# Ten idle products, an earlier gate, ScalarE as second asker for weights, and tables made by GpSimd, around the first routing of an attention and two-expert-layer kernel

## The chip, the cores and the metric

The kernel runs on one core of one Trainium2 chip. A core has TensorE (PE, matrix products; PEld is its loading of the stationary operand), VectorE (DVE), ScalarE (ACT), GpSimd (POOL) and SyncE (SP), which asks for most transfers. The metric is the time of one execution on the device in microseconds (us), as the median of several runs.

## The reference, cut to what matters

Attention over 2 x 8 heads of 576 tokens keeps the 32 largest scores of each row. Its output is an x of 1152 rows of 512. Two layers of eight experts follow, each with a gate that sends a row to one expert:

```python
logits = x @ w_gate
expert_idx = np.argmax(logits, axis=1)
...                                   # gate_w: the softmax value of the chosen expert
h = np.maximum(np.einsum('ecd,edf->ecf', disp, w1), 0.0)     # 512 -> 1024
y = np.einsum('ecf,efd->ecd', h, w2)                         # 1024 -> 512
...
        out[i] = gate_w[i] * y[expert_idx[i], pos[i]]
```

The first layer drops what an expert gets beyond its capacity of 288 rows; the second has no such limit. Only the routing depends on the data: which rows go to which expert.

## The kernel before, in words

**Stages.** Attention fills the first 249 us. At 249 us the first routing begins (`begin`, L1861): VectorE finds each row's expert and counts, experts are sorted by their number of rows, and rank 0 is the expert with most. From 256 us the first expert layer runs rank after rank, from about 412 us the second routing, and then the second expert layer to the end.

**Shapes.** The ranks of the first layer get 208, 192, 176, 160, 144, 128, 128 and 128 columns (L28), rows of x turned into columns. Rank 0 and 1 thus have two tiles of rows each (128 + 80 and 128 + 64), rank 2 has 128 + 48. What does not fit goes through a spill loop (`spill`, L1641) under a condition on a count `nblk` that every engine reads; the loop's code is jumped over when the count is zero.

**Form "S".** For ranks with more than 128 columns, weights and activations are split into a high part (ScalarE writes it, L1270 for weights) and a low part (VectorE subtracts, L1271), and TensorE makes a product with both parts (L1350, L1352 in the first layer of an expert, L1389, L1391 in the second). The result of one block f of 128 hidden columns goes back by ScalarE (`t`, L1322), VectorE (`s`, L1323), ScalarE (high part of `hT`, L1315) and VectorE (low part, L1316). There are eight f to an expert; the second product adds over all eight, so it wants `hT` of every f in turn. Weights reach the chip as `raw` tiles of 1 MB, two for w1 and two for w2 of an expert, in four buffers; their split copies are `w1c` and `w2c`.

**The early block.** One block of 128 rows of one expert was found during attention already. Its first layer (`early_hidden`, L1829) and second layer (`early_out`, L1838) are TensorE's work while the routing is computed elsewhere. Its gate value is made by `early_gate` (L1843, twelve small operations on GpSimd) and `early_sum` (L1856, one exponential on ScalarE over what `early_gate` left).

**Order.** Instructions of an engine run in the order in which the code is written; there is no scheduler. `layer1` (L1325) takes a list of side jobs and runs one of them ahead of each f from 1 to 7; other jobs, the splits of the weights, are handed along in the same list. In rank 0 the side jobs are: last early output and `early_sum`, `gate_in` (L1751), `next_places` (L1739, tables for the second routing), the rows of rank 1 with the request for its w1, and the early block's way out.

**Queues.** Weights are asked for by SP (L1229 for w1, L1241 for w2). Rows of x are fetched by indirect transfers that GpSimd issues (`bring`, L1212, instruction at L1218), into five `xr` buffers. GpSimd also writes the results `yr` of a rank to memory (L1773).

Of the kernel before, what the change touches and what calls it, by code (L numbers as in the profile page):

```python
# [16 lines left out]
OP = mybir.AluOpType  # L17
AX = mybir.AxisListType
PS = bass.MemoryType.PSUM
DR = bass.MemoryType.DRAM  # L20
SP = mybir.EngineType.SP

TOPK = 32
NEG = -1.0e30
# [9 lines left out]
NCOL = len(COLS[0])  # L34
# [19 lines left out]
def attn_moe_moe_kernel(ctx, tc, q, k, v, g1, w11, w12, capacity, g2, w21, w22, out):  # L54
    nc = tc.nc
# [4 lines left out]
    KF = F // 128  # L60
# [1099 lines left out]
    def moe(i, pools, src, lg, w1, w2, limit):  # L1160
# [5 lines left out]
        with ExitStack():  # L1166
# [7 lines left out]
            def new(shape, name, dt=F32):  # L1174
                return (consts if i == 0 and name in soonest else sm).tile(shape, dt, name=name)
# [54 lines left out]
                    got.append(raw)  # L1230
                return got

            def load_w2(e, late=False):
                w_ = w2[ds(e, 1)].rearrange("o (c p) f -> p (o c) f", p=128)
                got = []
                for h in range(2):
                    raw = wt.tile([128, KD, F // 2], F32, name="raw", bufs=4)
                    if late and h == 0:
                        nc.gpsimd.memset(raw[0:1, 0, 0:1], 0.0)
                    raw = raw.rearrange("p a b -> p (a b)").rearrange("p (c f) -> p c f", f=Dm)  # L1240
                    nc.sync.dma_start(raw, w_[:, h * KF // 2:(h + 1) * KF // 2])  # L1241
                    got.append(raw)
                return got

            def load_w2_apart(e):
                w_ = w2[ds(e, 1)].rearrange("o (c p) f -> p (o c) f", p=128)
                got = []
                for h in range(4):
                    raw = wt.tile([128, 2, Dm], F32R, name="w2c", bufs=12).bitcast(F32)
                    nc.sync.dma_start(raw, w_[:, h * KF // 4:(h + 1) * KF // 4])  # L1250
                    got.append(raw)
                return got
# [368 lines left out]
            def gate_rows():  # L1621
                tt(r3, isa[:, None].to_broadcast(b3), gcode[:, :, None, :].to_broadcast(b3), op=OP.mult)

            def chosen_one(r):
                return nc.values_load(eid0[0:1, 0:1] if i and r == 0 else eid[0:1, r:r + 1], engines=[SP], min_val=0,
                                      max_val=E - 1, skip_runtime_bounds_check_because="ranks are a permutation of the experts")

            def weights(r, j, gate=None):
                e = chosen_one(r)
                if j == 0:  # L1630
                    w1s[r] = [load_w1(e, gate=gate), {}]
                else:
                    w2s[r] = [load_w2_apart(e) if i == 0 and r == E - 1 else load_w2(e, i == 1 and r == 0), {}]

            def splits(r, j):
                w, form, f = ((w1s, form1, split_w1), (w2s, form2, split_w2))[j]
# [100 lines left out]
                        turn_out(yT, 0, 128, g, lambda yr: scatter(yr, 128, si, free=False))  # L1737

            def next_places():  # L1739
                okay = new([128, NCOL], "okay")  # L1740
                ts(okay, inv, 1.0, None, op0=OP.is_lt)
                for a, b, to in ((0, NCOL - 1, 0), (NCOL - 1, NCOL, LAST)):
                    ok, n = okay[:, a:b], b - a
                    cr = code[1][:, :, to:to + n]
                    stt(cr[:, 0], part.to_broadcast([128, n]), 64.0, ok, op0=OP.add, op1=OP.mult)
                    ts(cr[:, 1], iot[:, to:to + n], 128.0, -64.0, op0=OP.mult, op1=OP.add)
                    tt(cr[:, 1], cr[:, 1], ok, op=OP.mult)
                    bo = [128, n, E]
                    tt(revm[1][:, to:to + n], ok[:, :, None].to_broadcast(bo), rev[:, None, :].to_broadcast(bo), op=OP.mult)

            def gate_in():  # L1751
                pg = ps.tile([128, 512], F32, name="pi", bufs=1)
# [108 lines left out]
            def begin():  # L1861
                bank()
                choose(0, nch)
                early_hidden(0)
                count(0, nch)
                nc.scalar.activation(dl, dl, AF.Exp)
                none = new([128, 1], "none", U32)
                nc.gpsimd.memset(none, 0)
                yr = wk.tile([128, RW], F32, name="yr", bufs=3)
                gather(yr[:16, :Dm], none[:16])  # L1870
                two.prepare()
                for f in range(1, 5):
                    early_hidden(f)
                early_hidden(5, 0, KD // 2)
                weave(*ranking())
                weights(0, 0)
                assign()
                for j in range(2):
                    bring(j)
                for f in table["later"]:  # L1880
                    f()
                spill()
                weights(0, 1)
                for a, (r, t, m) in enumerate(cols):
                    if 0 < r < 3:
                        bring(a)
                early_gate()
                first_split = splits(0, 0)
                for f in first_split[:2]:
                    f()  # L1890
                yTs[-1] = wk.tile([128, KD, ny], F32, name="yT")
                early_out(0, 0, KF)
                early_out(1, 0, KF)
                xTs[0] = wk.tile([128, KD, 2, MOST], F32R, name="xT")
                for k, q in enumerate(tiles_of(0)):
                    rows_in(0, *q)
                for f in first_split[2:6]:
                    f()
                early_out(2, 0, KF)
                first_split[6]()  # L1900
                table["left"] = first_split[7:]
# [123 lines left out]
            def run(nxt=None):  # L2025
                if i == 0:
                    begin()
                rest = {0: splits(0, 1)}
                for r in range(E):
                    hTs[r] = wk.tile([128, KF, 2, MOST], F32R, name="hT", bufs=1)  # L2030
                    jobs, more_ = side(r, nxt), rest[r]
                    if i and r == 0:
                        more_ = [lambda p=p: [(split_high if p < 4 else split_low)(k) for k in w2_order[p]]
                                 for p in range(len(w2_order))]
                    if i == 0 and r == 0:
                        more_ = [lambda p=p, m=more_: [m[k]() for k in p] for p in
                                 ((), (0,), (1,), (2, 3), (4,), (5, 6), (7,))]
                    jobs = [(lambda p=p: [f() for f in p]) for p in
                            [jobs[k:k + 1] + more_[k:k + 1] for k in range(max(len(jobs), len(more_)))]]
                    layer1(form1[r], *w1s[r], xTs[r], hTs[r], sizes[r], form2[r] != "N", jobs)  # L2040
                    if r + 1 < E:
                        if r + 1 not in w1s:
                            weights(r + 1, 0)
                        weights(r + 1, 1)
                    if r + 3 < E:
                        for t, m in tiles_of(r + 3):
                            bring(first[r + 3] + t)
                    early, rest[r + 1] = splits(r + 1, 0), splits(r + 1, 1)
                    n_ = max(0, 11 - len(early))
                    if form2[r] == "R" and len(tiles_of(r)) == 1:  # L2050
                        n_ = KH
                    early, rest[r + 1] = early + rest[r + 1][:n_], rest[r + 1][n_:]
                    if i and r == 0:
                        early += [lambda q=q: rows_in(1, *q) for q in tiles_of(1)]
                    if form2[r] != "R":
                        yTs[r] = wk.tile([128, KD, ny], F32, name="yT")
                    each = end = None
                    kept_, place, put = [], ("pp", 4), rows(r)
                    if i and r == E - 1:
                        place = "pl", 1  # L2060
                        put = lambda *a: kept_.append(a)
                    if i and r == 0:
                        def each(d):
                            if d < 0:
                                gate_in()
                                place_of(0)
                                place_of(1)
                    if nxt and r == E - 1:
                        each, end = ending(yTs[r])
                        early += nxt.later()  # L2070
                    layer2(form2[r], *w2s[r], hTs[r], yTs.get(r), sizes[r], tiles_of(r), put, early, each, place)
                    if end:
                        nxt.late(end(nxt.ready, nxt.begun))
                    if r + 2 < E and form1[r + 1] != "N":
                        weights(r + 2, 0)
                if i:
                    spill()
                    for a in kept_:
                        rows(E - 1)(*a)
# [46 lines left out]
```

## Time and profile before

| what | value |
|---|---|
| median of 3 runs | 593.14 us (592.06 to 596.36) |
| profiled execution, its own time | 593.53 us |
| its span, first to last instruction | 591.9 us |
| mean granted TensorE clock | 0.99 |
| busy: PE / PEld / DVE / ACT / POOL | 572.0 / 542.8 / 476.5 / 418.7 / 263.9 us |
| DMA | 100.76 MB, mean 170 GB/s |

The time of an execution holds 1.6 us more than the span, work before the first and after the last instruction. Busy time of TensorE counts a product from its start to a modelled end, and products overlap, so a stretch where PE is all busy can still run at half the clock; the granted clock has to be read beside it.

### The profile page before, as it was taken

The numbers are of one execution on the slowest core, as the hardware profiler recorded it, in microseconds if no ns is written. First come the engines' busy times: TensorE is split into PE (matmuls) and PEld (weight loads), VectorE is DVE, ScalarE is ACT, GpSimd is POOL, SyncE is SP. The second block draws the span as 40 slices with busy tenths as digits, with TensorE's granted clock in tenths as the row PEclk, the third lists the DMA queues.
The fourth block names the chain that finished last, engine by engine and source line by source line (L and its number), as shares of the span: only waits on it lengthen the run. The fifth ranks groups of instructions, "written<-read, shape, count | busy, mean of one in ns | idle before, by whom it ended". The sixth has DMA issues, their size and how long they took to land.

```text
span 591.9 us, 13975 instructions
## 1 busy us (share of the span) xinstructions
PE 572.0 (97%) x4781; PEld 542.8 (92%) x4781; DVE 476.5 (81%) x1597; ACT 418.7 (71%) x1040; POOL 263.9 (45%) x590
## 2 busy tenths in 40 slices
PE   8999999999999999879999999999999999999994
PEld 5799999999999999779899999998998899999994
DVE  6999999999999999656878868642598688788750
ACT  6789998989898977427677777552365577878651
POOL 7768888988898797544220111010103302221010
PEclk9999999999999999989999989999999999999998
DMA  6530513161470190164987757786677767778660
GB/s 145 138 81 3 167 43 114 43 144 24 127 95 23 36 271 19 43 222 149 317 271 278 235 181 269 220 263 231 203 268 237 267 221 244 258 236 280 213 215 14
DMA packets 85168, 100.76 MB, mean 170 GB/s; under 512 B 33925, under 2 KB 46725, under 8 KB 85088
## 3 DMA queue, kind: packets, MB, share of 16 engines
q1 hardware_dynamic: 80160, 88.79, 48.6%
q0 software_dynamic: 3728, 10.70, 5.8%
q8 instruction: 40, 0.66, 0.5%
q10 hardware_dynamic: 1200, 0.30, 0.2%
q14 instruction: 40, 0.33, 0.2%
HBM read 86.51 MB, written 13.74 MB: 169 GB/s over the span
## 4 chain that ended last, share of the span: by engine, by line
PE 31%; DMA 10%; issue 7%; DVE 3%; POOL 1%; ACT 1%; POOLq 0%; SPq 0%; DVEq 0%; ACTq 0%
DMA out_dram<-yr,sidx 8%; PE pp L1389 6%; PE pp L1350 6%; PE pp L1336 3%; PE pp L1352 3%; PE pp L1391 3%; DMA raw<-in_moe_w_dram 1%; DVE w2c L1271 1%; PE pt L1300 1%; PE pl L1403 1%; PE pp L1385 1%; PE pp L1387 1%; PE pp L1386 1%; PE pp L1838 1%; PE pt L1440 1%
## 5 line engine op out<-in xcount | busy, mean ns | idle before, releaser
L1350 PE MATMUL pp<-xT,w1c 128*128 128x352 f32 (+4 forms) x316 | 94.3, 367 | 0.4 <-DVE xT L1306 0.4
L614 PE MATMUL xb<-vx,pT 128*128 128x73 f32 (+1 forms) x800 | 94.2, 266 | 0.5 <-ACT pT L602 0.3
L1271 DVE TENSOR_TENSOR w2c<-raw,w2c 128x512 fp32r<-128x512 f32 x112 | 74.5, 684 | 22.1 <-ACT w2c L1270 21.2
L1389 PE MATMUL pp<-hT,w2c 128*128 128x416 f32 (+4 forms) x320 | 89.5, 357 | 1.9 <-DVE hT L1316 1.9
L614 PEld LDWEIGHTS xb<-vx,pT 128*128 128x128 f32 (+1 forms) x800 | 87.1, 181 | 2.9 <-issue 1.3
L1391 PE MATMUL pp<-hT,w2c 128*128 128x208 f32 (+4 forms) x320 | 77.9, 244 | 0.0
L1352 PE MATMUL pp<-xT,w1c 128*128 128x176 f32 (+4 forms) x316 | 77.4, 245 | 0.0
L1270 ACT ACTIVATE w2c<-raw 128x512 fp32r<-128x512 f32 x112 | 67.2, 623 | 10.3 <-DMA raw<-in_moe_w_dram 6.9
L593 PE MATMUL pt<-ident,shifted 128*128 128x128 f32 x350 | 67.4, 278 | 0.0
L1389 PEld LDWEIGHTS pp<-hT,w2c 128*128 128x128 f32 x320 | 60.1, 188 | 4.3 <-DVE hT L1316 4.1
L594 PE MATMUL pt<-negid,under 128*128 128x128 bf16 x350 | 63.4, 219 | 0.5 <-ACT under L584 0.5
L1322 ACT ACTIVATE t<-pp 128x208 f32<-128x208 f32 (+4 forms) x120 | 37.2, 311 | 37.3 <-PE pp L1352 24.7
L1271 DVE TENSOR_TENSOR w1c<-raw,w1c 128x512 fp32r<-128x512 f32 x88 | 55.9, 685 | 8.2 <-ACT w1c L1270 7.8
L1350 PEld LDWEIGHTS pp<-xT,w1c 128*128 128x128 f32 x316 | 60.2, 190 | 1.8 <-DVE xT L1306 0.8
L1352 PEld LDWEIGHTS pp<-xT,w1c 128*128 128x128 f32 x316 | 61.2, 194 | 0.0
L1391 PEld LDWEIGHTS pp<-hT,w2c 128*128 128x128 f32 x320 | 61.1, 191 | 0.0
L1452 POOL DMA_INDIRECT out_dram<-yr,sidx x14 | 13.6, 973 | 103.3 <-ACT yr L1433 100.7
L1773 POOL DMA_DIRECT2D y<-yr x13 | 7.5, 575 | 113.7 <-issue 63.1
L584 ACT ACTIVATE under<-s,nb 128x576 bf16<-128x576 f32 x70 | 55.0, 787 | 1.4 <-POOL nb L576 1.3
L513 DVE MAX8 top<-ypair 128x8 f32<-128x160 f32 x192 | 54.2, 309 | 0.0
L587 POOL TENSOR_SCALAR shifted<-s,nb 128x576 f32<-128x576 f32 x70 | 52.1, 744 | 3.9
L593 PEld LDWEIGHTS pt<-ident,shifted 128*128 128x128 f32 x350 | 49.2, 140 | 3.5
(415 smaller groups left out, 1544.9 us busy)
## 6 DMA issues: line engine op xcount, KB each, us to landing
raw<-in_moe_w_dram SPq DMA_DIRECT2D x62, 1024.0 KB, 5.6
w1c<-in_moe_w_dram SPq DMA_DIRECT2D x8, 512.0 KB, 5.8
y<-blank SPq DMA_DIRECT2D x1, 2308.5 KB, 20.4
out_dram<-blank SPq DMA_DIRECT2D x3, 768.0 KB, 4.7
y<-yr POOLq DMA_DIRECT2D x8, 256.5 KB
kraw<-in_k_dram SPq DMA_DIRECT2D x8, 256.0 KB, 2.9
vraw<-in_v_dram SPq DMA_DIRECT2D x16, 128.0 KB, 2.9
vx<-in_v_dram SPq DMA_DIRECT2D x16, 128.0 KB, 2.8
```

Source lines behind the costliest of these rows:

```text
L513: ops.append(lambda w=w, cur=cur: nc.vector.max(w, cur))
L584: nc.scalar.activation(under[k % 3][:, :S], s, AF.Relu, bias=nb[:, 1:2], scale=-BIG)
L587: nc.gpsimd.tensor_scalar(shifted[k % 3][:, :S], s, nb[:, 0:1], 1.0, op0=OP.add, op1=OP.mult)
L593: both = (nc.tensor.matmul(pt[:, o], shifted[k % 3][:, o], ident, is_transpose=True, start=True, stop=False), nc.tensor.matmul(pt[:, o], u ...
L594: nc.tensor.matmul(pt[:, o], under[k % 3][:, o], negid, start=False, stop=True))
L614: nc.tensor.matmul(o, pT[:, c2, cols], z["v"][:, c2, hh], start=(c2 == 0), stop=(c2 == NC - 1))
L1270: nc.scalar.activation(o[:, 0], src_, AF.Copy)
L1271: nc.vector.tensor_tensor(o[:, 1], src_, o[:, 0].bitcast(F32), op=OP.subtract)
L1350: nc.tensor.matmul(ph[:, :2 * n].rearrange("p (w n) -> p w n", w=2), w[f][:, 0, d], xT[:, d, :, :n], start=st, stop=False)
L1352: nc.tensor.matmul(ph[:, :n], w[f][:, 1, d], xT[:, d, 0, :n], start=False, stop=sp)
L1389: nc.tensor.matmul(py[:, :2 * n].rearrange("p (w n) -> p w n", w=2), w[f][:, 0, o], hT[:, f, :, :n], start=st, stop=False)
L1391: nc.tensor.matmul(py[:, :n], w[f][:, 1, o], hT[:, f, 0, :n], start=False, stop=sp)
```

## The change

It touches the first routing and rank 0 of the first expert layer, in five places. (1) Ten products of 64 columns whose result nobody reads are put ahead of the ranking. (2) `early_gate` moves ahead of the fetches of rank 1's rows on GpSimd. (3) w2 of rank 0 is asked for by ScalarE, behind its first two splits, instead of SP. (4) `next_places` moves from VectorE to GpSimd, with one operation more (`up`). (5) The fetches of rank 2's rows move from the routing to behind rank 0's first layer, ahead of those of rank 3, and the splits of rank 0's w2 begin one side job sooner.

```diff
-            def load_w2(e, late=False):
+            def load_w2(e, late, queue):
...
-                    nc.sync.dma_start(raw, w_[:, h * KF // 2:(h + 1) * KF // 2])
+                    queue.dma_start(raw, w_[:, h * KF // 2:(h + 1) * KF // 2])
...
             def next_places():
-                okay = new([128, NCOL], "okay")
-                ts(okay, inv, 1.0, None, op0=OP.is_lt)
+                okay, up = new([128, NCOL], "okay"), new([128, 1], "up")
+                g = nc.gpsimd
+                g.tensor_scalar(okay, inv, 1.0, 1.0, op0=OP.is_lt, op1=OP.mult)
+                g.tensor_scalar(up, part, 64.0, 1.0, op0=OP.add, op1=OP.mult)
...
-                    stt(cr[:, 0], part.to_broadcast([128, n]), 64.0, ok, op0=OP.add, op1=OP.mult)
-                    ts(cr[:, 1], iot[:, to:to + n], 128.0, -64.0, op0=OP.mult, op1=OP.add)
-                    tt(cr[:, 1], cr[:, 1], ok, op=OP.mult)
+                    g.tensor_tensor(cr[:, 0], up.to_broadcast([128, n]), ok, op=OP.mult)
+                    g.tensor_scalar(cr[:, 1], iot[:, to:to + n], 128.0, -64.0, op0=OP.mult, op1=OP.add)
+                    g.tensor_tensor(cr[:, 1], cr[:, 1], ok, op=OP.mult)
...
                 early_hidden(5, 0, KD // 2)
+                spin(10, 64)
                 weave(*ranking())
...
                 spill()
-                weights(0, 1)
-                for a, (r, t, m) in enumerate(cols):
-                    if 0 < r < 3:
-                        bring(a)
                 early_gate()
+                for t in range(len(tiles_of(1))):
+                    bring(first[1] + t)
                 first_split = splits(0, 0)
                 for f in first_split[:2]:
                     f()
+                weights(0, 1, eng=ACT)
...
-                                 ((), (0,), (1,), (2, 3), (4,), (5, 6), (7,))]
+                                 ((0,), (1,), (2,), (3, 4), (5,), (6,), (7,))]
...
-                    if r + 3 < E:
-                        for t, m in tiles_of(r + 3):
-                            bring(first[r + 3] + t)
+                    for r_ in (r + 2, r + 3)[r > 0 or i > 0:]:
+                        for t, m in tiles_of(r_):
+                            bring(first[r_] + t)
```

GpSimd between the spill loop's end and the first result that it writes, before (`e_` are the early gate's numbers, `xr` fetched rows, `y` the results in memory):

```order
L1218 DMA xr<-x,gidx 128x512
L1218 DMA xr<-x,gidx 64x512
L1218 DMA xr<-x,gidx 128x512
L1218 DMA xr<-x,gidx 48x512
L1847 TENSOR_SCALAR e_inv<-early 128x1
...
L1853 TENSOR_SCALAR e_max<-e_max 128x1
L1859 TENSOR_SCALAR e_sum<-e_sum 128x1
L1772 COPY yr<-tokf 128x1
L1773 DMA y<-yr 128x513
L1218 DMA xr<-x,gidx 128x512
L1218 DMA xr<-x,gidx 32x512
```

and now (lines are shifted by one to three):

```order
L1850 TENSOR_SCALAR e_inv<-early 128x1
...
L1856 TENSOR_SCALAR e_max<-e_max 128x1
L1219 DMA xr<-x,gidx 128x512
L1219 DMA xr<-x,gidx 64x512
L1862 TENSOR_SCALAR e_sum<-e_sum 128x1
L1743 TENSOR_SCALAR okay<-inv 128x14
...
L1752 TENSOR_TENSOR revm_107<-okay,rev 128x8
L1775 COPY yr<-tokf 128x1
L1776 DMA y<-yr 128x513
L1219 DMA xr<-x,gidx 128x512
L1219 DMA xr<-x,gidx 48x512
```

The gate stands ahead of the fetches, the ten operations of the tables stand between the gate's sum and the first written result, and the fetches of rank 2 (128 and 48 rows) stand behind that result.

ScalarE from the end of the spill loop to the early gate's exponential (`e_ex`), now:

```order
L1271 ACTIVATE w1c<-raw 128x512 x2
L1626 TENSOR_LOAD eid
L1242 ISA
L1242 DMA raw<-in_moe_w_dram 128x4x512
L1242 ISA
L1242 DMA raw<-in_moe_w_dram 128x4x512
L1844 ACTIVATE yT<-pp 128x128 x2
...
L1271 ACTIVATE w1c<-raw 128x512
L1861 ACTIVATE e_ex,e_sum<-early,e_max 128x8
L1271 ACTIVATE w2c<-raw 128x512
L1323 ACTIVATE t<-pp 128x208
```

Before, the five rows of the request were not there, and between `e_ex` and `t` stood no split.

VectorE in the first layer of rank 0, from the last split of w1, before:

```order
L1271 TENSOR_TENSOR w1c<-raw,w1c 128x512
L1323 TENSOR_TENSOR s<-pp,t 128x208
L1316 SCALAR_TENSOR_TENSOR hT<-s,hT 128x208
...
L1741 TENSOR_SCALAR okay<-inv 128x14
L1745 SCALAR_TENSOR_TENSOR code_109<-part,okay 128x13
...
L1749 TENSOR_TENSOR revm_107<-okay,rev 128x8
L1271 TENSOR_TENSOR w2c<-raw,w2c 128x512
```

The nine operations from `okay` to the second `revm` are gone from VectorE, and a first split of w2 (`w2c`) stands between the last split of w1 and the `s` that followed it.

## Rows read from the trace of the kernel before

**Rows 1.** Waits of TensorE, 246-592 us: waiter, releaser, us, times, longest.

```profile
PE pp L1838 <- PEq L1644: 3.2, 1, 3.2
PE pp L1389 <- DVE hT L1316: 1.9, 5, 0.6
...
PE pi L1573 <- DVE r L1554: 0.4, 1, 0.4
```

**Rows 2.** Queue instructions of L1644, 258-262 us: ns min/median/max, starts.

```profile
L1644 PEldq COMPARE_BRANCH  x1: 2990/2990/2990, 258.4 to 258.4; - x1
```

**Rows 3.** The same at the second layer's spill loop, 560 to 592 us.

```profile
L1644 PEldq COMPARE_BRANCH  x1: 345/345/345, 580.5 to 580.5; - x1
```

**Rows 4.** Stretches: busy us of PE, PEld, DVE, ACT, POOL; clock; DMA; GB/s.

```profile
259.00:262.40 3.40, 0.65 (x6) 0.69 (x7) 1.84 (x4) 1.15 (x2) 2.42 (x4) 1.00 1.04 380
262.40:265.80 3.40, 3.40 (x19) 3.40 (x18) 0.00 (x0) 0.28 (x1) 0.76 (x1) 0.50 0.76 205
...
276.20:288.30 12.10, 10.86 (x74) 9.82 (x72) 11.69 (x38) 9.96 (x27) 1.99 (x4) 1.00 0.45 164
```

**Rows 5.** Timeline of TensorE, routing: start, us, operation, count [idle before <-releaser].

```profile
250.61 0.42 PE L1525 MATMUL pl<-oh,ones 128*128 128x80 bf16 x10
```

**Rows 6.** Timeline of TensorE, the early block's second layer.

```profile
261.75 5.44 PE L1838 MATMUL pp<-w2c,w1c 128*128 128x128 f32 x32 [3.16 <-PEq L1644]
```

**Rows 7.** The same, its last quarter, 268 to 282 us.

```profile
270.89 1.96 PE L1838 MATMUL pp<-w2c,w1c 128*128 128x128 f32 x16
```

**Rows 8.** Timeline of TensorE, second layer of rank 0.

```profile
284.23 0.26 PE L1352 MATMUL pp<-xT,w1c 128*128 128x208 f32 x1
284.32 0.37 PE L1389 MATMUL pp<-hT,w2c 128*128 128x416 f32 x1
...
285.54 0.37 PE L1389 MATMUL pp<-hT,w2c 128*128 128x416 f32 x1
...
288.33 0.46 PE L1389 MATMUL pp<-hT,w2c 128*128 128x416 f32 x1
```

**Rows 9.** Timeline of TensorE, rank 2's rows in the first layer of rank 1.

```profile
297.14 0.60 PE L1300 MATMUL pt<-ident,xr 128*128 128x128 f32 x4
```

**Rows 10.** Timeline of GpSimd, 255 to 400 us.

```profile
259.56 0.95 POOL L1218 DMA_INDIRECT xr<-x,gidx  x1 [0.37 <-issue]
...
267.89 0.88 POOL L1218 DMA_INDIRECT xr<-x,gidx  x1 [4.73 <-PE pt L1300]
268.85 0.25 POOL L1847 TENSOR_SCALAR e_inv<-early 128x1 f32<-128x1 f32 x1
...
271.20 1.27 POOL L1852 TENSOR_SCALAR e_max<-early 128x1 f32<-128x1 f32 x1
...
286.05 0.67 POOL L1773 DMA_DIRECT2D y<-yr  x1 [9.54 <-ACT w2c L1270]
```

**Rows 11.** Timeline of ScalarE and VectorE, 268 to 282 us.

```profile
273.06 0.62 ACT L1270 ACTIVATE w1c<-raw 128x512 fp32r<-128x512 f32 x1
...
275.56 0.30 ACT L1858 ACTIVATE e_ex<-early,e_max 128x8 f32<-128x8 f32 x1 [1.88 <-POOL e_max L1853]
...
276.22 0.37 DVE L1323 TENSOR_TENSOR s<-pp,t 128x208 f32<-128x208 f32 x1 [1.80 <-ACT t L1322]
...
278.36 0.17 DVE L1741 TENSOR_SCALAR okay<-inv 128x14 f32<-128x14 f32 x1
...
279.46 0.16 DVE L1749 TENSOR_TENSOR revm<-okay,rev 128x8 f32<-128x8 f32 x1
```

**Rows 12.** Timeline of SP's requests, 248 to 292 us.

```profile
265.44 0.94 SPq L1241 DMA_DIRECT2D raw<-in_moe_w_dram  x2
281.54 1.02 SPq L1229 DMA_DIRECT2D raw<-in_moe_w_dram  x2
```

**Rows 13.** DMA queues, 257 to 261 us: packets, MB, share of 16 engines.

```profile
q1 hardware_dynamic: 780, 1.56, 102.7%
```

**Rows 14.** The same, 261 to 265 us.

```profile
q0 software_dynamic: 318, 1.00, 84.6%
```

More of the change, by code (lines that the diff above doesn't have):

```diff
@@ L21 @@
 SP = mybir.EngineType.SP
+ACT = mybir.EngineType.Activation
 TOPK = 32
@@ L1622, in gate_rows, with chosen_one, weights @@
                 tt(r3, isa[:, None].to_broadcast(b3), gcode[:, :, None, :].to_broadcast(b3), op=OP.mult)
-            def chosen_one(r):
-                return nc.values_load(eid0[0:1, 0:1] if i and r == 0 else eid[0:1, r:r + 1], engines=[SP], min_val=0,
+            def chosen_one(r, eng=SP):
+                return nc.values_load(eid0[0:1, 0:1] if i and r == 0 else eid[0:1, r:r + 1], engines=[eng], min_val=0,
                                       max_val=E - 1, skip_runtime_bounds_check_because="ranks are a permutation of the experts")
-            def weights(r, j, gate=None):
-                e = chosen_one(r)
+            def weights(r, j, gate=None, eng=SP):
+                e = chosen_one(r, eng)
                 if j == 0:
@@ L1632, in weights @@
                 else:
-                    w2s[r] = [load_w2_apart(e) if i == 0 and r == E - 1 else load_w2(e, i == 1 and r == 0), {}]
+                    w2s[r] = [load_w2_apart(e) if i == 0 and r == E - 1 else load_w2(e, i == 1 and r == 0, nc.sync if eng == SP else nc.scalar), {}]
             def splits(r, j):
@@ L1744, in next_places @@
                     cr = code[1][:, :, to:to + n]
-                    stt(cr[:, 0], part.to_broadcast([128, n]), 64.0, ok, op0=OP.add, op1=OP.mult)
-                    ts(cr[:, 1], iot[:, to:to + n], 128.0, -64.0, op0=OP.mult, op1=OP.add)
-                    tt(cr[:, 1], cr[:, 1], ok, op=OP.mult)
+                    g.tensor_tensor(cr[:, 0], up.to_broadcast([128, n]), ok, op=OP.mult)
+                    g.tensor_scalar(cr[:, 1], iot[:, to:to + n], 128.0, -64.0, op0=OP.mult, op1=OP.add)
+                    g.tensor_tensor(cr[:, 1], cr[:, 1], ok, op=OP.mult)
                     bo = [128, n, E]
-                    tt(revm[1][:, to:to + n], ok[:, :, None].to_broadcast(bo), rev[:, None, :].to_broadcast(bo), op=OP.mult)
+                    g.tensor_tensor(revm[1][:, to:to + n], ok[:, :, None].to_broadcast(bo), rev[:, None, :].to_broadcast(bo), op=OP.mult)
             def gate_in():
```

## Prediction, made before the changed kernel ran

> **What bounds the kernel now.** I read the waits of TensorE first, since the change touches a stretch where TensorE nearly always has work. From the start of the routing to the end it waits in few places [rows 1]: once for 3.2 us on its own queue at the spill loop, and some 1.9 us in all for `hT` of an expert's second layer; it waits 0.4 us for the table `r` of the routing. Each is read at its place. The queue's wait is one branch of 2.99 us [rows 2]; the same branch takes 0.345 us behind the second layer [rows 3]. After it TensorE runs at a granted clock of 0.50, the 1.2 GHz level, for one stretch [rows 4]; in the stretch before it had been busy 0.65 of 3.40 us. The 32 products of the early block that fall there take 5.44 us [rows 6], the 16 of its last part at 2.4 GHz 1.96 us [rows 7], so 3.92 for 32: the half clock costs 1.5 us.
>
> The waits for `hT` are the interesting ones, and the timeline of TensorE in rank 0's second layer sizes them [rows 8]. f = 0 starts at 284.32 and f = 4 at 285.54, 0.305 us a step. f = 7 would start at 286.45 at that step and starts at 288.33: **1.88 us lost**. Why VectorE is late with `hT` shows in its timeline and in the stretch from 276.2 to 288.3, where it is busy 11.69 of 12.10 us [rows 4]: it works off a backlog. The backlog begins at 276.22, with a wait of 1.80 us for ScalarE [rows 11]. ScalarE had ended a split at 273.68 (273.06 + 0.62) and stood 1.88 us at the early gate's exponential `e_ex`, which waits for GpSimd's `e_max`. GpSimd was late since the gate's operations stood behind a row fetch that waited 4.73 us for a free buffer [rows 10]. Into the backlog fall the tables of `next_places`, from 278.36 to 279.62: 1.26 us of VectorE.
>
> **The early gate ahead of the fetches.** Its twelve operations took from 268.85 to 275.53, 6.7 us or 0.56 each [rows 10, 11]. Started behind the spill loop at about 259.6, where the first of the moved fetches stood [rows 10], they end by 266.3, 7 us before ScalarE reaches `e_ex`. The 1.88 us of ScalarE go, and with them VectorE's 1.80: of that time VectorE spends part on the first split of w2, which the change puts there and which it had to do later before.
>
> **The tables to GpSimd.** VectorE loses 1.26 us of work. With 1.80 that is some 3.0 us, more than the 1.88 that TensorE lost, so the backlog is gone before f = 7, and what is late next is the chain behind rank 0's last first-layer product. It ends at 284.49 (284.23 + 0.26) [rows 8]. Four steps follow (`t`, `s`, two of `hT`); at the 0.37 us of `s` [rows 11] they end at 285.97. ScalarE may have one split of 0.62 ahead of them: 286.6. So f = 7 starts between 286.45 and 286.7, against 288.33: a gain of 1.6 to 1.9. **I take 1.6**, the end at which the split does stand in the way; the bounds are 0, if something else is late by as much, and 1.88.
>
> On GpSimd the ten operations cost 5.6 us at 0.56 each. They run from about 274.5, when `e_sum` is done, to 280.1, inside the 9.54 us that GpSimd stood idle before it wrote the early block's result [rows 10]. That result can be written at about 284.4 now, 1.7 earlier with the backlog gone. Cost: nothing; if each took the 1.27 us of the slowest of the early gate's [rows 10], 12.7 us, the write would go 3 us late, and the fetches behind it (a rival below). `e_inv` took 0.25 us when VectorE was not splitting weights, the 1.27 us one ran beside splits. The Trainium skill's GPSIMD Engine Reference, Specifications, says that GpSimd's way into SBUF is shared with VectorE and contended when VectorE reads two SBUF inputs, as the splits do. By that rule the tables stay slow for as long as VectorE splits; the sum by it is the same as by the 0.56 of the rows, and only the rival's chance rises.
>
> **Rank 1's rows** are now fetched from about 266.3, 6.7 us later. No packet of GpSimd's fetches moved from 257 to 261 us, while the weights' queue filled 102.7% of the engines [rows 13], though the first fetch was out by then; from 261 to 265 they had 84.6% [rows 14]. So a fetch waits for the weights that were asked for before it. Ahead stand w2's 2.1 MB, from about 262; at the 0.38 MB/us of a full stretch [rows 4] they are in by 268, the 0.4 MB of rows by 269.5. They are wanted as the third side job, after 276.22. Cost: nothing.
>
> **w2 by ScalarE.** SP asked at 265.44 [rows 12], after the spill loop's joins; ScalarE asks behind two splits, at about 262. Two requests hold an engine 0.94 us; ScalarE is busy only 0.28 of the 3.40 us from 262.4 [rows 4], so this is hidden. The weights come 3.5 us sooner, and at 5.5 us for 2.1 MB they would have come by 272 anyway, ahead of the first split at about 274: worth nothing by itself.
>
> **The ten idle products.** The nearest row is ten products of 8 to 80 columns, 44 in the mean, in 0.42 us [rows 5]; by columns, ten of 64 take up to 0.6. They fill the 0.4 us in which TensorE waits for `r`. What is left, 0 to 0.2 us, comes ahead of the 2.99 us branch. I take 0.
>
> **Rank 2's rows** are fetched behind the early block's written result, so at about 285 instead of 262 and 268. Ahead of them stand rank 1's w1, asked for at 281.54 before [rows 12] and some 2 us sooner now, and its w2: 4.2 MB from 280 are in by 291, the written block's 0.26 MB and the rows' 0.36 MB by 292.7. TensorE wanted them at 297.14 [rows 9], now 295.4. Hidden, with under 3 us to spare.
>
> **Sum.** 593.53 us of the profiled execution less 1.6 are 591.9. That execution stands 0.4 over the median of 593.14, so the forecast for a median is **591.5**. The gain should last: TensorE's waits behind it are short, and weights and splits follow its progress.
>
> **Rivals**, all as medians.
>
> 1. The branch gets short. The changed stream has twenty instructions more ahead of it, and the branch has two lengths in this trace [rows 2, 3]. That would give back 2.65 us and, without the long idle time ahead, the 1.5 of the half clock: 587.4; half of it, 589.5. Against it: the DMA engines are as full at 258 us as before, since nothing of the change comes earlier. Chance 0.13.
>
> 2. Nothing is gained. ScalarE, which now has a split between `e_ex` and `t` and one more wait behind it, hands `t` on as late as before, or TensorE meets a further stretch of half clock (the one here cost 1.5): 593.1. For it: such stretches need not fall alike in every run. Chance 0.15.
>
> 3. Slower by the fetches. GpSimd's ten tables beside VectorE's splits take 12.7 us, the write and rank 2's fetches go out 3 us late, and rank 2's w1 gets ahead of them. This decides once the first fetch goes out later than about 289. Another 2.1 MB are 5.5 us: the rows come at about 298, TensorE waits 2.5 us at 295.4, and perhaps runs at half clock for 1.5: 594.0 to 595.5. Against it: 0.56 is the mean even of operations beside splits. The Trainium skill's page DMA: Bandwidth & Descriptors, Issuing engines are not separate DMA queues, has transfers of all askers interleave; by it the rows would not wait for w1 at all and this rival would have a chance of 0.02. The row of 257 to 261 us does not agree, and it decides. Chance 0.07.
>
> 4. Slower by code. TensorE's instructions come by DMA too; a block of them that is wanted just behind the branch would now stand behind w2, asked for 3.5 us sooner. Nearest row: another branch's 2.99 us: 594.5, with half clock 596.0. Against it: TensorE ran through full stretches of DMA without such a wait. Chance 0.07.
>
> **Numbers.** The forecast has 0.58, with 590.4 to 592.6 for its own: a gain of 0.9 to 1.9 and some tenths of run to run. The range goes from **588.0 to 594.5**: it leaves out the full length of rival 1 and the far ends of 3 and 4, 0.16 in all. One per cent, 5.9 us, is about what a measurement of this kernel tells from no change; faster by that needs all of rival 1 and a little more, 0.05; slower by that needs more than any rival gives, 0.02; within it, 0.93.
>
> **What would show it.** Right: `e_ex` starts within 0.3 us of the split ahead of it; VectorE has no wait over 1 us at the first `s` behind it; TensorE's waits for `hT` at rank 0 are under 0.4 us. The branch at 258.4 is still about 3 us and half clock follows. Wrong: a wait of TensorE at rank 2's rows, a short branch, or waits for `hT` as long as they were.

## The result, and the profile after

The changed kernel takes **587.80 us** (median of 20 runs, 586.30 to 592.16) against 593.35 for the kernel before (20 runs, 591.67 to 597.78): 5.55 us less, a ratio of 0.9901 with a 95% interval of 0.9882 to 0.9921. The forecast was 591.5, with a range down to 588.0, so the time lies just below the range. Rival 1, the branch that gets short, was priced at 587.4.

The profiled execution of the changed kernel took 590.42 us, 2.6 over its median, with a span of 588.8. Its attention part ended 0.98 us later than in the profile of before. Stages are therefore compared from the routing's own start, in each profile by itself. Lines of the changed kernel are one to three higher than those of before.

The waits of TensorE come first again, same columns as [rows 1]:

```profile
PE pp L1841 <- issue: 1.1, 1, 1.1
PE pt L1447 <- ACT yr L1434: 0.9, 1, 0.9
...
PE pp L1390 <- DVE hT L1317: 0.7, 3, 0.2
PE pt L1301 <- DMA xr<-x,gidx: 0.6, 1, 0.6
```

The wait of 3.2 us on TensorE's queue has become 1.1, the longest wait for `hT` is 0.2 us, and the 0.4 for `r` does not appear. New are 0.6 us for rank 0's rows and 0.9 for ScalarE's `yr`. The branch behind the routing, in the view of [rows 2], with ScalarE's execution of the same branch:

```profile
L1645 PEldq COMPARE_BRANCH  x1: 425/425/425, 259.4 to 259.4; - x1
L1645 ACTq COMPARE_BRANCH  x1: 45/45/45, 260.4 to 260.4; - x1
```

2990 ns have become 425. TensorE's timeline around it answers [rows 5, 6]:

```profile
250.50 1.16 PE L1832 MATMUL pp<-blank,w1c 128*128 128x128 f32 x8 [0.80 <-ACTq L1055]
...
251.90 4.25 PE L1832 MATMUL pp<-blank,w1c 128*128 128x128 f32 x36
255.99 0.46 PE L1464 MATMUL pp<-idle,ones 128*128 128x64 bf16 x10
256.51 0.73 PE L1574 MATMUL pi<-r,onehot 128*128 128x28 bf16 x10
257.08 2.48 PE L1832 MATMUL pp<-blank,w1c 128*128 128x128 f32 x20
260.66 3.84 PE L1841 MATMUL pp<-w2c,w1c 128*128 128x128 f32 x32 [1.09 <-issue]
264.33 0.60 PE L1301 MATMUL pt<-ident,xr 128*128 128x128 f32 x4
265.51 0.47 PE L1301 MATMUL pt<-ident,xr 80*128 80x80 f32 x4 [0.58 <-DMA xr<-x,gidx]
```

From the routing's first product to the table products (L1574) it is 6.01 us, as before: the idle products fill the wait for `r` and cost no time. The 32 products behind the branch take 3.84 us, where [rows 6] has 5.44, and 1.09 us of waiting ahead of them instead of 3.16. The stretches with the branch and the products behind it (columns as in [rows 4]) show a full clock in both, and VectorE 11.06 of 12.10 us busy later:

```profile
259.98:263.38 3.40, 2.72 (x24) 2.73 (x25) 1.85 (x4) 1.15 (x2) 3.03 (x8) 1.00 1.01 373
263.38:266.78 3.40, 2.82 (x27) 2.61 (x27) 0.99 (x2) 1.84 (x5) 2.49 (x8) 1.00 0.79 232
277.20:289.30 12.10, 12.10 (x85) 11.72 (x84) 11.06 (x27) 10.16 (x25) 5.26 (x6) 1.00 0.91 322
```

Rank 0's second layer, and rank 2's rows in the first layer of rank 1, as in [rows 8, 9]:

```profile
282.36 0.36 PE L1390 MATMUL pp<-hT,w2c 128*128 128x416 f32 x1
...
284.58 0.46 PE L1390 MATMUL pp<-hT,w2c 128*128 128x416 f32 x1
...
293.39 0.60 PE L1301 MATMUL pt<-ident,xr 128*128 128x128 f32 x4
```

The rows shown first and second are f = 0 and f = 7: 2.22 us apart, where seven steps of 0.305 make 2.13. The 1.88 us that were lost there have become 0.09. ScalarE runs the early gate's exponential right behind a split, with no wait:

```profile
271.14 0.62 ACT L1271 ACTIVATE w1c<-raw 128x512 fp32r<-128x512 f32 x1
271.66 0.29 ACT L1861 ACTIVATE e_ex<-early,e_max 128x8 f32<-128x8 f32 x1
```

GpSimd, answering [rows 10]:

```profile
265.00 0.19 POOL L1856 TENSOR_SCALAR e_max<-e_max 128x1 f32<-128x1 f32 x1
265.35 1.06 POOL L1219 DMA_INDIRECT xr<-x,gidx  x1
...
272.66 0.82 POOL L1743 TENSOR_SCALAR okay<-inv 128x14 f32<-128x14 f32 x1
...
276.44 0.34 POOL L1752 TENSOR_TENSOR revm<-okay,rev 128x8 f32<-128x8 f32 x1
...
282.82 0.67 POOL L1776 DMA_DIRECT2D y<-yr  x1 [5.91 <-ACT w2c L1271]
283.79 1.11 POOL L1219 DMA_INDIRECT xr<-x,gidx  x1 [0.30 <-issue]
```

**The sum by stages.** From the table products' start (255.53 before, 256.51 after) to f = 7 of rank 0 it was 32.80 us and is 28.07: **4.73 us less**. It is made of 2.07 (the wait ahead of the first product behind the branch, 3.16 to 1.09), 1.60 (full clock, 5.44 to 3.84), 1.79 (`hT`, 1.88 to 0.09), less 0.58 for rank 0's rows and 0.15 of small differences. From there to the span's end it is 303.57 us before and 304.22 after, so 0.65 are given back in these two executions; "Left open" below shows that this is a difference of two larger figures.

When did the block of instructions behind the branch move? The profile has a DMA queue for instructions, q8, that moves one packet of 0.02 MB at a time. That it is TensorE's is inferred: in each of the five kernels with a long branch, a packet started 0.3 to 0.9 us behind the branch's start and the branch ended 2.4 to 2.5 us behind the packet's start. In the kernel before it starts in this quarter of a microsecond, 258.75 to 259.0 (queue, packets, MB, share of 16 engines):

```profile
q1 hardware_dynamic: 51, 0.10, 103.3%
q8 instruction: 1, 0.02, 27.6%
```

In the changed kernel it starts between 254.75 and 255.0, alone, 4.6 us ahead of the branch:

```profile
q8 instruction: 1, 0.02, 24.0%
```

And from 257 to 259.4 the weights fill the engines as much as before:

```profile
q1 hardware_dynamic: 479, 0.97, 105.1%
```

So the engines are no emptier at the branch; the block was in before they filled.

The profiles of e1 to e4 and e12 below are of executions 1.1 to 2.0% above the fastest of their kernel (e1 and e3 the furthest), so only counts from inside the stage are taken from them.

### The profile page after: what moved, and what is told of

It is laid out like the page before. It is cut to its first block, busy times and chain, and to the rows that moved or that the text cites. A ratio compares the mean times of both kernels' runs of the same rounds, so it can differ in the third digit from the quotient of the medians.

```text
span 588.8 us, 14001 instructions
## 1 busy us (share of the span) xinstructions
PE 569.0 (97%) x4791; PEld 539.5 (92%) x4791; DVE 476.0 (81%) x1588; ACT 417.9 (71%) x1040; POOL 266.5 (45%) x600
## 4 chain that ended last, share of the span: by engine, by line
PE 33%; DMA 11%; issue 7%; DVE 3%; ACT 1%; POOL 0%; POOLq 0%; DVEq 0%; SPq 0%; ACTq 0%
DMA out_dram<-yr,sidx 8%; PE pp L1351 7%; PE pp L1390 6%; PE pp L1353 3%; PE pp L1337 3%; PE pp L1392 3%; DMA raw<-in_moe_w_dram 1%; PE pl L1404 1%; PE pt L1301 1%; DMA xr<-x,gidx 1%; PE pp L1388 1%; PE pp L1386 1%; PE pp L1387 1%; DVE w2c L1272 1%; DMA xr<-y,gid 1%
## 5 line engine op out<-in xcount | busy, mean ns | idle before, releaser
L1351 PE MATMUL pp<-xT,w1c 128*128 128x352 f32 (+4 forms) x316 | 92.8, 361 | 0.7 <-DVE xT L1307 0.4
L1351 PEld LDWEIGHTS pp<-xT,w1c 128*128 128x128 f32 x316 | 59.5, 188 | 2.1 <-DVE xT L1307 0.9
L1353 PEld LDWEIGHTS pp<-xT,w1c 128*128 128x128 f32 x316 | 60.4, 191 | 0.0
```

The lines of the kernel that those rows point to most:

```text
L1351: nc.tensor.matmul(ph[:, :2 * n].rearrange("p (w n) -> p w n", w=2), w[f][:, 0, d], xT[:, d, :, :n], start=st, stop=False)
L1353: nc.tensor.matmul(ph[:, :n], w[f][:, 1, d], xT[:, d, 0, :n], start=False, stop=sp)
```

## The experiments

Each variant has one profiled execution; five were also timed in three rounds. "Block" is when TensorE's instruction block starts to move, counted from the table products' start; "f = 7" is rank 0's, counted likewise. The routing's first product started between 249.5 and 257.5 us in these profiles, hence the count from inside.

| kernel | block, us | branch, ns | f = 7, us |
|---|---|---|---|
| before | +3.37 | 2990 | 32.80 |
| changed | -1.75 | 425 | 28.07 |
| e1 idle products alone | -1.82 | 425 | 29.22 |
| e2 all but the idle products | +3.22 | 2765 | 30.74 |
| e3 ten at the routing's head | +3.19 | 2825 | 32.59 |
| e4 changed, tables on VectorE | -1.32 | 425 | 28.76 |
| e5 five | +3.38 | 2945 | 32.78 |
| e6 ten behind the table products | +3.74 | 3365 | 33.14 |
| e7 16 at the head | -2.64 | 337 | 28.76 |
| e8 ten of 8 columns | -1.62 | 337 | 29.60 |
| e9 weights asked for later | +0.47 | 425 | 38.42 |
| e10 12 at the head | -2.62 | 337 | 29.53 |
| e11 eight | -1.83 | 425 | 29.63 |
| e12 changed, fetches as before | -1.33 | 337 | 29.42 |

The 32 products behind the branch took 5.44 us (part of them at half clock) in the five kernels with a branch over 2.7 us, and 3.84 in all others.

**e1.** The kernel before with the idle products and nothing else.

```diff
                 early_hidden(5, 0, KD // 2)
+                spin(10, 64)
                 weave(*ranking())
```

> The kernel before with the ten idle products alone. Theory A (the twenty instructions more shift TensorE's code, so that the block behind the spill loop's branch is asked for before the branch): the branch takes under 0.5 us instead of 2.99, no half clock follows it, and the time falls by 2.6 + 1.5 = 4.1 us less up to 0.7 us of a new wait for rank 0's rows: about 589.6 us. Theory B (the branch got short through the other edits, which change what DMA carries): branch 3 us, half clock, time as before, 593.3.

```profile
L1644 PEldq COMPARE_BRANCH  x1: 425/425/425, 263.7 to 263.7; - x1
```

Ratio to before 0.9925 [0.9887, 0.9963]. f = 7 comes 3.58 us sooner. The ten products alone make the branch short and keep the clock; they were the term taken at 0. The 3.58 are not the branch and the clock alone: rank 0's rows make TensorE wait 1.05 us, and f = 0 to f = 7 takes 2.83 us (287.21 to 290.04), so only 0.70 of the 1.88 us are lost there, though neither the gate nor the tables were touched.

**e2.** The changed kernel without them.

```diff
                 early_hidden(5, 0, KD // 2)
-                spin(10, 64)
                 weave(*ranking())
```

> The changed kernel without the ten idle products. Theory A: the branch is back at about 3 us with half clock behind it; only the 1.5 to 1.9 us of the hT waits stay gained: 591.2 to 591.9 us. Theory B: the branch stays at 0.43 us, 587.8 us.

```profile
L1645 PEldq COMPARE_BRANCH  x1: 2765/2765/2765, 266.4 to 266.4; - x1
```

```profile
269.52 5.44 PE L1841 MATMUL pp<-w2c,w1c 128*128 128x128 f32 x32 [2.94 <-PEq L1645]
```

Branch and half clock are back; f = 7 still comes 2.06 us sooner than before, with f = 0 to f = 7 in 2.22 us (292.05 to 294.27) as in the changed kernel. The ratio is 0.9898 [0.9826, 0.9970], from four runs of 587.94 to 595.98 us: by whole times alone e2 would pass for as fast as the changed kernel, and they are too scattered to tell. In the stage the gate, the tables and the fetches are worth some 2 us by themselves. The two gains add up to 5.6 where both together gave 4.7, since either one takes a part of the same `hT` waits.

**e3.** The ten products at the head of the routing.

```diff
             def begin():
+                spin(10, 64)
                 bank()
```

> The kernel before with the same ten idle products six us earlier, at the head of the first routing, where TensorE waits anyway. Theory A (place does not matter, only the number of instructions ahead of the branch): branch under 0.5 us, no half clock, as the run with the products in the changed kernel's place, about 589.6 us. Theory C (the products matter as work in the 0.4 us gap ahead of the routing's table): branch 3 us, half clock, 593.3 us.

```profile
L1644 PEldq COMPARE_BRANCH  x1: 2825/2825/2825, 264.0 to 264.0; - x1
```

As many instructions, between the same two branches, and only 0.21 us are gained in the stage. (Its whole time came out at 0.9948 [0.9899, 0.9997] all the same, which shows how little the whole times can order these variants.)

**e4.** The changed kernel with the tables of `next_places` on VectorE as before.

```diff
-                g.tensor_scalar(okay, inv, 1.0, 1.0, op0=OP.is_lt, op1=OP.mult)
...
+                ts(okay, inv, 1.0, None, op0=OP.is_lt)
...
+                    tt(revm[1][:, to:to + n], ok[:, :, None].to_broadcast(bo), rev[:, None, :].to_broadcast(bo), op=OP.mult)
```

> The changed kernel with next_places back on VectorE. If the tables were part of VectorE's backlog: their 1.26 us come back as waits of TensorE for hT in rank 0's second layer, up to 1.2 us, time 588.5 to 589.0. If the earlier gate alone was enough to clear the backlog (VectorE has about 1.8 us to spare then): waits for hT under 0.3 us more, 587.8 to 588.1.

f = 7 comes 0.69 us later than in the changed kernel, and f = 0 to f = 7 loses 0.64 us (286.56 to 289.33) instead of 0.09; ratio to before 0.9948 [0.9904, 0.9992]. The move of the tables is worth about 0.6 us of the `hT` waits.

**e5 to e8** vary number, place and length of the idle products in the kernel before.

```diff
e5:              early_hidden(5, 0, KD // 2)
+                spin(5, 64)
e6:              places(a, nch)
+                if i == 0:
+                    spin(10, 64)
e7:          def begin():
+                spin(16, 64)
e8:              early_hidden(5, 0, KD // 2)
+                spin(10, 8)
```

> The kernel before with 5 idle products (10 wanted by the change) of 64 columns directly ahead of the table products. Theory place (any work between the 36 first-layer products and the table products' waits lets TensorE ask for its next block of instructions early): the branch behind the routing waits 0.4 us as with ten, the block comes some 4 us ahead of it, no stretch at half clock. Theory number (the code ahead of the branch must be longer by so many instructions): with half of them the branch still waits 2.8 to 3.0 us and the half clock follows (L1838 x32 5.4 us). Theory time (the table products must not be reached before r is there; r was waited for 0.36 us): five products last 0.25 us, the wait for r is some 0.1 us and the branch still waits 2.8 us.

> The kernel before with the ten idle products directly behind the table products (behind their waits, still ahead of the branch). Theory place: the waits are reached as early as in the kernel before, so the branch waits 2.8 to 3.0 us and half clock follows. Theory number: the same number of instructions between the two branches as with the ten ahead, so the branch waits 0.4 us. Theory time: the wait for r stays at 0.36 us and the branch waits 2.8 us.

> The kernel before with 16 idle products at the head of the routing (ten there left the branch at 2825 ns). Theory number: ten early ones fell one or a few instructions short, 16 are enough, and the branch waits 0.4 us. Theory place: they stand ahead of the first-layer products and not between these and the table products: the branch waits 2.8 us again.

> The kernel before with ten idle products of 8 columns instead of 64 at the change's place: as many instructions, less time. Theory place and theory number: the branch waits 0.4 us as with 64 columns. Theory time: the ten last less (0.3 us or less instead of 0.46), the wait for r is some 0.1 us or none; if the wait for r is what counts and it is still there, the branch waits 2.8 us.

In e5 and e6 the branch takes 2945 and 3365 ns, in e7 and e8 337. Theory place alone falls with e7: 16 products at the head do what ten there did not. Theory number as the count between the two branches falls with e6: ten behind the table products change nothing. Theory time falls with e7, which waits 0.37 us for `r` and has a short branch. What e1 to e8 agree with is a count of the instructions **ahead of the table products' waits**. Idle products also take one buffer of the `pp` ring, which shifts every later buffer; e5 and e6 shift it as e1 does and have a long branch, so that is not the cause.

**e9.** The kernel before, with the same instructions for TensorE, and rank 0's first-layer weights asked for only behind the branch.

```diff
                 weave(*ranking())
-                weights(0, 0)
                 assign()
...
                 spill()
+                weights(0, 0)
                 weights(0, 1)
```

> The kernel before, without idle products, with the request for the first expert's first-layer weights moved behind the branch on the request queue, so that no weights fill the DMA engines when TensorE reaches the table products and the branch. In the late kernels the block of instructions moved 3.2 to 3.5 us after the table products started. Theory held up (the block is asked for when the table products' waits clear, and stands behind the weights): it now moves within 1 us of the table products' start and the branch waits 0.4 us. Theory asked at the branch: it moves some 0.3 us after TensorE reaches the branch, 2.9 us or more behind the table products' start, and the branch still waits 2 to 3 us. The weights come late here, so the time of the whole kernel is some us longer under either.

The instruction queue from 259.75 to 260.0 (the table products start at 259.46), and the branch:

```profile
q8 instruction: 1, 0.02, 35.7%
```

```profile
L1644 PEldq COMPARE_BRANCH  x1: 425/425/425, 262.3 to 262.3; - x1
```

The block moves 0.47 us behind the table products' start and 2.4 us ahead of the branch. With the same instructions it came 2.9 us later in the kernel before, 0.5 us behind the branch's start, where the transfer of weights had just begun as the table products started. A request at the branch would fit the late kernels as well; e9 rules it out. So TensorE asks for the block at about the point where the table products' waits clear, and the weights delay it. Why by some 3 us, when the weights fill the engines until 261 us, no run shows. The late weights cost what was expected: asked for at 268.5 us, they make TensorE wait 7.1 us for the first product of rank 0 (the profile puts the wait down to `xT`):

```profile
277.50 0.54 PE L1343 MATMUL pp<-xT,w1c 128*128 128x208 f32 x1 [7.14 <-ACT xT L1303]
```

The Trainium skill's page Runtime: NRT & Kernel Launch, Instruction fetch mechanics, says that each sequencer asks for its next block, of 256 instructions, by its own DMA queue at fixed boundaries in the program while it still executes the current one, and that this is mostly hidden. The trace agrees on the first part, with one packet of 0.02 MB at a time and a point that moves with the number of instructions; on the second it does not where a weight transfer fills the engines: 2.6 us of the branch showed.

**e10, e11.** Twelve at the head, eight at the change's place.

```diff
e10:         def begin():
+                spin(12, 64)
e11:             early_hidden(5, 0, KD // 2)
+                spin(8, 64)
```

> The kernel before with 12 idle products at the head of the routing (10 there left the branch at 2825 ns, 16 there made it 0.4 us). Counted from the head of this stretch of the program, the table products' waits are instruction 115 in the kernel before, 120 and more with five idle products, 134 with ten early ones, 135 with ten at the change's place, 146 with 16 early ones (waits, weight loads and products counted, an FP32 product as four). Theory number (TensorE asks for its next block when its sequencer, which runs ahead up to those waits, has passed a fixed place in the code between 134 and 135): at 138 the branch waits 0.4 us and there is no half clock. Theory place: 2.8 us as with ten.

> The kernel before with eight idle products at the change's place instead of ten. Theory number: the waits stand at 131 and so ahead of the place in the code: the branch waits 2.8 to 3.1 us and the half clock follows. Theory that the cover of the wait for r is what counts (five products of 64 columns left 0.22 us of it, ten none): with eight the wait is under 0.1 us and the branch waits 0.4 us.

```profile
L1644 PEldq COMPARE_BRANCH  x1: 337/337/337, 265.2 to 265.2; - x1
```

```profile
L1644 PEldq COMPARE_BRANCH  x1: 425/425/425, 265.6 to 265.6; - x1
```

Both are short (the first row is e10, the second e11). e10 is as theory number had it, e11 is not: by my count its waits are instruction 131, and those of e3, where the block came late, are 134. Either the count misses some instructions or the place has a small part in it. At the change's place the point lies between five and eight products, at the head between 10 and 12; the exact rule stays open.

The products at the head also reach the second layer's spill loop. Its branch on TensorE's weight queue takes 3480 ns in e7 and 3860 in e10, against 337 to 345 in the twelve other kernels, and it ends 2.3 to 2.5 us behind the start of an instruction packet there too (580.41 and 584.17 us). TensorE's last product ends at about the same time as the branch, so nothing is lost there; but instructions that are added ahead of one branch can make a later one long.

**e12.** The changed kernel with the fetches of ranks 1 and 2 ahead of the gate again, as before.

```diff
                 spill()
+                for a, (r, t, m) in enumerate(cols):
+                    if 0 < r < 3:
+                        bring(a)
                 early_gate()
-                for t in range(len(tiles_of(1))):
-                    bring(first[1] + t)
...
-                    for r_ in (r + 2, r + 3)[r > 0 or i > 0:]:
-                        for t, m in tiles_of(r_):
-                            bring(first[r_] + t)
+                    if r + 3 < E:
+                        for t, m in tiles_of(r + 3):
+                            bring(first[r + 3] + t)
```

> The changed kernel with the row fetches of ranks 1 and 2 asked for where they were before (ahead of the early gate), rank 3's behind rank 0's first layer; the rest as changed. Forecast's own term: the early gate's sum comes some 1.9 us later again, ScalarE's backlog behind it comes back and rank 0's hT waits with it (1.2 to 1.9 us), so 1 to 2 us slower than the changed kernel, 588.8 to 589.8 against 593.35. Rival: with the branch short and the tables on GpSimd there is no backlog to clear: hT waits stay under 0.5 us and the time is the changed kernel's.

f = 7 comes 1.35 us later than in the changed kernel (ratio to before 0.9937 [0.9888, 0.9986]), the size expected, but by another way than expected. A fetch waits for a buffer again and ScalarE stands at `e_ex` again:

```profile
271.41 0.89 POOL L1219 DMA_INDIRECT xr<-x,gidx  x1 [2.47 <-PE pt L1301]
```

```profile
278.79 0.30 ACT L1861 ACTIVATE e_ex<-early,e_max 128x8 f32<-128x8 f32 x1 [1.19 <-POOL e_max L1856]
```

but TensorE's waits for `hT` stay at 0.7 us in all, three of them: f = 0 to f = 7 takes 2.56 us, 0.43 over seven steps. That VectorE has no tables to make fits this; it was not tried apart. The rest, some 0.9 us, is lost earlier, in a longer wait for rank 0's own rows (1.22 and 0.20 us for its two tiles, against 0.58):

```profile
270.51 0.63 PE L1301 MATMUL pt<-ident,xr 128*128 128x128 f32 x4 [1.22 <-DMA xr<-x,gidx]
```

w2 asked for by ScalarE was not tried alone, so its part of the 2 us is open.

## Why the prediction was wrong, point by point

- **The ten idle products: the step that failed.** The forecast took them at 0, and rival 1 with a chance of 0.13 because "the DMA engines are as full at 258 us as before, since nothing of the change comes earlier". The engines are as full (105.1% from 257 to 259.4), but what matters is when TensorE asks for its block, not how full they are at the branch. With the ten products ahead of the waits it asks 1.75 us ahead of the table products, into empty engines; without them at the table products, just as the weights start. e1 and e2 show that it is these products, e9 that the weights are what delays the block. The change did not make that transfer later or smaller, it let the request out before it. The price was nearly right: 4.15 us in rival 1, 3.67 measured (2.07 and 1.60). At f = 7 it is 3.2 to 4.0 in e1, e7, e8, e10 and e11, with a part of the `hT` waits gone and new waits for rank 0's rows in it.
- **2.65 us for the branch** was 0.6 too much: the queue instruction is 2.57 us shorter, but the first product behind it comes only 2.07 sooner, since ScalarE, to which the profile of e1 puts the wait down, reaches the same branch at 260.4, some 0.6 us after TensorE is through. That it is ScalarE which holds the product back is read from that profile; no run took the wait away.
- **1.5 us for the half clock** was right: 1.60. Half clock follows the long wait behind the branch in every variant that has it, and is absent there in every one without it.
- **The gate and the tables, 1.6 of at most 1.88**, were right: 1.79 measured, and 2.22 us from f = 0 to f = 7 in e2 too. `e_ex` starts behind its split, and no wait of VectorE for ScalarE from 274 to 284 is over 0.7 us. The tables' part is 0.6 (e4). The mechanism was drawn too simply: with a standstill of 1.19 us at `e_ex` back but the tables gone, only 0.43 us are lost (e12), and with the branch short but gate and tables as before, 0.7 to 1.2 instead of 1.88 (e1, e7, e8, e10, e11).
- **The tables on GpSimd** were forecast to run 5.6 us from 274.5 and ran 4.1 (272.66 to 276.78), beside VectorE's splits of w2; the slow 1.27 us one of before has no like here, the longest is 0.82; the early block's result went out at 282.82, not 284.4. Rival 3 fell: rank 2's rows, fetched from 283.79, are there at 293.39 without a wait.
- **Rank 1's rows** were fetched at 265.35 (forecast 266.3), and TensorE did not wait for them. That a fetch waits for the weights asked for before it holds: its first packets moved some 1.7 us after GpSimd issued it where no weights were on the way (e9, 260.88 to 262.6), and 4.2 us after in the kernel before (256.96 to 261.2). **w2 by ScalarE** was asked for at 262.98 and held ScalarE 1.30 us, not 0.94; it is hidden. Rival 4 fell with it: no branch waits behind w2.
- **Not foreseen:** with TensorE 3.7 us earlier behind the branch, rank 0's own rows are late by 0.58 us. And there is a new wait of 0.94 us near the end of the first layer's ranks:

```profile
391.83 0.65 PE L1447 MATMUL pt<-ident,yr 128*128 128x128 f32 x4 [0.94 <-ACT yr L1434]
```

- **Left open:** what the change is worth behind rank 0. The kernel before has one more stretch at half clock, which the changed one has not (columns as in [rows 4]; the first row is before, the other two span the same work after):

```profile
344.30:347.70 3.40, 3.40 (x17) 3.40 (x16) 1.09 (x4) 1.73 (x4) 0.03 (x1) 0.50 0.64 245
```

```profile
338.00:342.00 4.00, 4.00 (x39) 3.96 (x38) 3.12 (x12) 2.13 (x7) 0.00 (x0) 1.00 0.63 201
342.00:346.00 4.00, 4.00 (x33) 3.98 (x33) 2.78 (x9) 3.50 (x10) 1.89 (x4) 1.00 0.41 150
```

Counted from the table products, the changed kernel is 4.68 us ahead when TensorE turns rank 4's rows (339.39 before, 335.69 after) and 6.24 at rank 5's (360.55 and 355.29). To the end it loses 2.16 of these again, 0.94 in the wait above and the rest in smaller steps. The profiles' gain from the routing to the end, 4.08 us, thus holds 1.56 for a stretch that is not shown to come from the change: profiles of e1 and e4 have one at 344 to 350 us and those of e11 and e12 at 326 to 332 although their branch is short, and e2 with its long branch has none. How often the timed runs had such a stretch is not known, so of the 5.55 us between the medians (interval 4.7 to 7.0) only the stage's 4.73 is accounted for.

## What to carry to other kernels

A long branch on TensorE's queue is a late block of instructions: look in the DMA view for when that block moved, and for what filled the engines between the last wait ahead of the branch and the branch. If a weight transfer starts there, it can be beaten in two ways that these runs show: more instructions ahead of that wait (eight short products did), or a later transfer (which cost more than it gave here). Price an edit that adds instructions by the instruction fetches too, not only by its own time, and look at every later branch as well; and when whole times scatter by a per cent, time the stage from a fixed instruction inside it.

## What the runs showed of the hardware

- TensorE's next block of instructions can be asked for well ahead of the branch that needs it (it moved 2.4 us ahead in e9, 4.6 in the changed kernel), and waits in the program can hold the request back: counted from the table products, it moved at -2.64 to -1.32 us, at +0.47 or at +3.19 to +3.74 us in these kernels.
- One packet of instructions, about 1 us long (24.0% of 16 engines in a quarter of a microsecond), started 3.2 to 3.7 us behind the table products where a weight transfer began with them; with idle engines it started 0.47 us behind (e9). A branch that waited for it ended 2.3 to 2.5 us behind its start, seven times.
- A wait of TensorE of 2.9 to 3.2 us at the branch was followed by half clock every time (five kernels), one of 1.1 us there never (nine). A wait is not the only thing that precedes half clock: in the kernel before, the clock was 0.50 from 344.30 to 347.70 us with TensorE busy 2.00 of 2.00 us in both stretches ahead of it (340 to 344).
- Whole times follow the mean granted clock of a run in the main: the unchanged kernel took 597.6 us at a mean of 0.983 and 591.6 at 0.995, though also 599.5 at 0.989.
